# Re-cutting a routing pass into segments of 6, 5, 5, 5 and 3 blocks beside an attention kernel's half blocks

## The chip, the cores and the metric

The program runs on one core of one Trainium2 chip. The metric is the device time of one execution in microseconds, given as the median of a few executions. A core has five engines with in-order queues of their own: TensorE (PE in the profile, with its weight loads as PEld), VectorE (DVE), ScalarE (ACT), GpSimd (POOL) and SyncE (SP, which here only issues DMAs). They wait for each other through semaphores.

## The reference

The reference is a windowed attention followed by a mixture of experts. What the change touches is the routing between the two:

```python
logits = x @ w_gate
noisy_logits = logits + np.log1p(np.exp(x @ w_noise)) * noise
top2 = np.argpartition(-noisy_logits, 2, axis=1)[:, :2]      # two of 8 experts per token
for e in range(E):
    for k in range(2):
        mask = top2[:, k] == e
        h = np.maximum(x[mask] @ w1[e], 0.0)
        out[mask] += top2_w[mask, k, None] * (h @ w2[e])
```

There are 3072 tokens of 512 features (4 batches of 768, with 8 heads of 64), 8 experts and 1024 inner features.

## The kernel before

Attention goes over 24 blocks of 128 tokens. A block is done in two half blocks of four heads each, so there are 48 half blocks; half block 0 is the first. In each of them the main loop emits, in this order: `score` of the next half block (L837 on VectorE, then the exponentials L840 on ScalarE), the transposes of the attention weights (L853 on TensorE, the first TensorE work of a half block, by which the text tells them apart), `gate_t` in even half blocks (GpSimd's copies L235 of the block's finished rows, and TensorE's transposes L371), the next score products (L823), `norm` (L885, L887, L890 on VectorE), `attend` (L874 on TensorE) and `gate_l` (L393 on TensorE). A block's gate logits are ready two blocks after its attention.

Routing is a generator, `route(r)`, one for each segment of blocks in `SEG`. It is a chain of some forty short VectorE operations on tiles of at most 128x96: softplus, top two (L479, L481), one-hot marks of the chosen experts, then a running count on TensorE. The count takes, for each block of the segment, a product with a strictly upper triangular matrix (L526) and one product with ones for each earlier block (L528), and one more per block for the total (L530). From the count come each token's row and tile within its expert. `mask(i)` makes two 128x128 0/1 matrices for block i (L555), `marks(i)` makes two 128x168 tables of token number and weight (L583, one for each of the two choices), and L608 multiplies the two into PSUM; L611 adds that to the table `tab`, from which expert token lists are read.

The steps of these generators are put between the attention's instructions by `tick`, which is called seven times in a half block (four times inside `score`, three times inside `norm`) and takes one step each time, and by `finish` at the end of the half block, which takes up to five steps of the third segment (`CLOSE` = 2) and later ones, and up to three of the first two. A step that yields True, 2 or LAST keeps the generator waiting until a later place. The third segment closes expert 0's first 512 rows: as soon as it is done, four gathers (L243, GpSimd) fetch these tokens, GpSimd copies them into whole words (L235, tile `xg`), and `turn` transposes them (L338) for expert 0's first products (L1107). Segments 3 and 4 are finished among those products: the generator `late` (segment 3) and `last` (segment 4) are advanced at 32 fixed slots of expert 0's first layer, and after them `rank` sorts the experts and starts the next gathers. Masks are made by GpSimd up to the third segment and by VectorE after it.

## Time and profile before

| | us |
|---|---|
| median of 3 runs (718.05 to 721.97) | 720.09 |
| the profiled execution | 719.72 |
| its span, first to last instruction | 718.0 |

| engine | busy us | share of the span |
|---|---|---|
| PE | 692.9 | 97% |
| PEld | 618.7 | 86% |
| DVE | 456.1 | 64% |
| ACT | 439.3 | 61% |
| POOL | 320.0 | 45% |

The attention's half blocks fill the span from 7 us to about 160 us. Expert 0's first layer begins at 165 us, and the other seven experts follow from 242 us to the end. TensorE's granted clock is 1.00 of full speed all through the attention. A matmul's record lasts longer than its share of TensorE, since matmuls overlap: what a run of them costs is read from start to start.

### The profile page before, as it was taken

How to read it: one execution, taken by the hardware profiler on the slowest of the kernel's cores; microseconds unless marked ns; L12 is line 12 of the kernel's file. 1: busy time of each engine (PE TensorE's matmuls, PEld its weight loads, DVE VectorE, ACT ScalarE, POOL GpSimd, SP SyncE). 2: the span in 40 equal slices, each digit the busy share in tenths (PEclk: the TensorE clock that was granted, in tenths of full speed). 3: DMA queues.
4: the chain of work that ended last, by engine and by line, in shares of the span. 5: the costliest groups of instructions: out<-in, count | busy, mean ns of one | idle time of the engine just before them, and what ended most of it. 6: DMA issues, size and time to landing. Idle time of an engine off the chain costs nothing.

```text
span 718.0 us, 16228 instructions
## 1 busy us (share of the span) xinstructions
PE 692.9 (97%) x5769; PEld 618.7 (86%) x5769; DVE 456.1 (64%) x1473; ACT 439.3 (61%) x922; POOL 320.0 (45%) x416
## 2 busy tenths in 40 slices
PE   7999999999999799999899999999999999999995
PEld 5888888787789699999799999999899899889984
DVE  7669888967946467736563676567466756756600
ACT  6888787653328397546664586478558646845511
POOL 3363626472087371064517461644465344533222
PEclk9999999999999999999999999999999999999998
DMA  9986779684098783156915692668458646943233
GB/s 257 345 259 219 215 234 297 194 304 182 0 253 176 167 141 118 16 114 167 202 30 98 172 225 45 133 170 167 75 126 193 128 107 167 206 73 89 31 45 47
DMA packets 129913, 111.10 MB, mean 155 GB/s; under 512 B 51578, under 2 KB 96762, under 8 KB 129824
## 3 DMA queue, kind: packets, MB, share of 16 engines
q1 hardware_dynamic: 118416, 83.84, 42.3%
q0 software_dynamic: 11264, 25.89, 19.8%
q8 instruction: 47, 0.77, 0.5%
q10 hardware_dynamic: 144, 0.26, 0.2%
q14 instruction: 42, 0.34, 0.1%
HBM read 71.07 MB, written 27.59 MB: 137 GB/s over the span
## 4 chain that ended last, share of the span: by engine, by line
PE 69%; DVE 8%; issue 8%; POOL 6%; DMA 5%; ACT 3%; POOLq 0%; SPq 0%; ACTq 0%; DVEq 0%
PE bank L1397 23%; PE av L1144 20%; PE av L1167 7%; PE av L874 4%; PE sc L823 4%; PE at L853 3%; DMA xt<-xg 2%; PE at L1107 1%; POOL out_dram L1120 1%; POOL xt L235 1%; DVE wall L196 1%; DVE ns L837 1%; POOL xg L243 1%; DMA xg<-xd,ids 1%; PE sc L1107 1%
## 5 line engine op out<-in xcount | busy, mean ns | idle before, releaser
L1397 PE MATMUL bank<-xh,wall 128*128 128x384 f32 (+4 forms) x784 | 215.6, 343 | 0.2
L1397 PEld LDWEIGHTS bank<-xh,wall 128*128 128x128 f32 x784 | 143.5, 188 | 5.0 <-DVE wall L196 1.6
L1397 PE MATMUL bank<-xl,wall 128*128 128x384 f32 (+4 forms) x392 | 133.4, 340 | 0.0
L1144 PE MATMUL av<-w2h,hh 128*128 128x512 f32 x304 | 120.3, 396 | 4.8 <-ACT hh L1088 2.5
L1120 POOL DMA_INDIRECT out_dram<-y,ids x40 | 64.0, 1599 | 126.0 <-ACT y L1117 122.3
L1144 PE MATMUL av<-w2h,hl 128*128 128x512 f32 x304 | 119.4, 393 | 0.1
L1144 PE MATMUL av<-w2l,hh 128*128 128x512 f32 x304 | 119.1, 392 | 0.0
L196 DVE TENSOR_TENSOR wall<-raw,wall 128x512 fp32r<-128x512 f32 (+1 forms) x84 | 73.6, 882 | 48.4 <-ACT wall L195 48.2
L1092 DVE SCALAR_TENSOR_TENSOR hl<-bank,hh 128x384 fp32r<-128x384 f32 (+4 forms) x84 | 47.1, 561 | 64.0 <-ACT hh L1088 62.9
L195 ACT ACTIVATE wall<-raw 128x512 fp32r<-128x512 f32 (+1 forms) x84 | 58.2, 701 | 43.4 <-POOL raw L1252 43.4
L243 POOL DMA_INDIRECT xg<-xd,ids x53 | 56.6, 1067 | 52.5 <-DVE place L293 32.4
L840 ACT ACTIVATE a<-ns,mx 128x168 f32<-128x168 f32 (+1 forms) x192 | 67.9, 422 | 19.4 <-DVE mx L837 18.7
L1397 PEld LDWEIGHTS bank<-xl,wall 128*128 128x128 f32 x392 | 73.9, 188 | 2.7
L1144 PEld LDWEIGHTS av<-w2h,hh 128*128 128x128 f32 x304 | 57.1, 188 | 14.8 <-ACT hh L1088 3.0
L1144 PEld LDWEIGHTS av<-w2h,hl 128*128 128x128 f32 x304 | 57.1, 188 | 13.3 <-DVE hl L1092 0.8
L275 ACT ACTIVATE xg<-xt 128x1024 uint16<-128x1024 uint16 (+3 forms) x46 | 59.4, 1312 | 11.7 <-DMA xt<-xg 11.7
L1144 PEld LDWEIGHTS av<-w2l,hh 128*128 128x128 f32 x304 | 57.1, 188 | 9.4 <-DVE w2l L196 0.3
L837 DVE CUSTOM_DVE_ANT_0 ns<-sc,bias 128x168 f32<-128x168 f32 (+1 forms) x188 | 51.7, 318 | 18.5 <-PE sc L823 13.5
L1251 POOL TENSOR_TENSOR raw<-raw 128x256 f32<-128x256 f32 x28 | 21.8, 779 | 90.3 <-DVE wall L196 90.2
L1088 ACT ACTIVATE hh<-bank 128x384 fp32r<-128x384 f32 (+4 forms) x84 | 42.0, 500 | 31.3 <-DVE bank L1467 23.8
L235 POOL COPY xt<-y 128x256 uint16<-128x256 uint16 x96 | 35.2, 404 | 50.8 <-DVE y L890 50.8
L874 PE MATMUL av<-vs,at 128*64 128x65 f32 (+1 forms) x768 | 57.3, 224 | 0.0
(214 smaller groups left out, 1484.4 us busy)
## 6 DMA issues: line engine op xcount, KB each, us to landing
raw<-in_w SPq DMA_DIRECT2D x64, 256.0 KB
raw<-in_w SPq DMA_DIRECT2D x32, 512.0 KB
out_dram<-zero SPq DMA_DIRECT2D x14, 512.0 KB
vs<-in_v SPq DMA_DIRECT2D x24, 260.0 KB
xd<-xt SPq DMA_DIRECT2D x24, 256.0 KB
qbuf<-in_q SPq DMA_DIRECT2D x23, 256.0 KB
ks<-in_k SPq DMA_DIRECT2D x20, 272.0 KB
vp<-in_v SPq DMA_DIRECT2D x20, 195.0 KB
```

The costliest lines, as they stand in the source:

```text
L195: nc.scalar.activation(hi, src, AF.Copy)
L196: eng.tensor_sub(lo, src, hi.bitcast(F32))
L243: nc.gpsimd.indirect_dma_start(out=xg[e, t].bitcast(U16)[:m], out_offset=None, in_=xd[:n], in_offset=bass.IndirectOffsetOnAxis(ap=r, axis= ...
L275: nc.scalar.activation(words(x), xt.pop((e, t)).rearrange("p (h k) t -> p h (k t)", h=2), AF.Copy)
L837: nc.vector.tensor_tensor_reduce(out=ns[x][:, s, :w], in0=ps[:, s], in1=bias[:, u + x, s] if i else bias0[:, u + x, s], scale=-scale, scal ...
L840: nc.scalar.activation(A[n + x][:, s * w:(s + 1) * w], ns[x][:, s, :w], AF.Exp, bias=mx[x][:, s:s + 1], scale=-1.0)
L874: nc.tensor.matmul(ps[s * Q:(s + 1) * Q, h], a[r:z, part * P + q0:part * P + q0 + Q], t[r:z, c], start=k == 0 and (n == 1 or h == 0), stop ...
L1092: nc.vector.scalar_tensor_tensor(lo, src, 0.0, hi.bitcast(F32), op0=OP.max, op1=OP.subtract)
L1120: ins = nc.gpsimd.indirect_dma_start(out=out, out_offset=bass.IndirectOffsetOnAxis(ap=r, axis=0), in_=y, in_offset=None, bounds_check=N + ...
L1144: nc.tensor.matmul(ps, x[j][:, f, cols], w[:, f], start=n == 0, stop=n == 3 * FC - 1)
L1167: nc.tensor.matmul(to, w[:, f, cols], x[:, f], start=n == 0, stop=n == 3 * FC - 1)
L1397: nc.tensor.matmul(ps, wb[c % 2][u][:, 2 * a + k], x[v][:, 2 * b + k], start=start and n == 0, stop=stop and n == 5, skip_group_check=True)
```

## The change

1. The segments are 6, 5, 5, 5 and 3 blocks instead of 6, 6, 5, 4 and 3. The second and the third segment end one block (two half blocks) earlier; the fourth has one block more.
2. A cap, `PACE`, is set back at the start of each half block: at most 4 steps of segment 0, 5 of segment 1 and 8 of segment 2 are taken in it, by `tick` and `finish` together. Segments 3 and 4 have no cap.
3. The count takes one product with the triangular matrix over all blocks of the segment and then, for d = 1 to w, one product with ones whose output is shifted by d blocks: 1 + w products for a segment of w blocks, whose outputs grow to 48 columns.
4. `marks(i)` makes both tables of a block in one operation of 128x336.
5. The first three segments have one group of marks each (all masks, all marks, then all products), where the first two had two groups of three blocks. All masks come before the wait for the marking of the segment before, and the ring of masks has 12 buffers instead of 5. The third segment's masks are made by VectorE instead of GpSimd.

```diff
-    SEG = [(0, 6), (6, 12), (12, 17), (17, 21), (21, NT)]
+    SEG = [(0, 6), (6, 11), (11, 16), (16, 21), (21, NT)]
...
-        for i in range(w):
-            nc.tensor.matmul(pos[:, i], upper, ohs[:, i], start=True, stop=i == 0)
-            for j in range(i):
-                nc.tensor.matmul(pos[:, i], ones, ohs[:, j], start=False, stop=j == i - 1)
-        for j in range(w):
-            nc.tensor.matmul(tot, ones, ohs[:, j], start=j == 0, stop=j == w - 1)
+        of = ohs.rearrange("p t e -> p (t e)")
+        nc.tensor.matmul(ps[:, :w * E], upper, of, start=True, stop=False, skip_group_check=True)
+        for d in range(1, w + 1):
+            nc.tensor.matmul(ps[:, d * E:(w + 1) * E], ones, of[:, :(w + 1 - d) * E], start=False, stop=d == w,
+                             skip_group_check=True)
...
-            m = wts.tile([P, 2, P], FR, name="m", bufs=5)
+            m = wts.tile([P, 2, P], FR, name="m", bufs=12)
-                (nc.vector if r > CLOSE else nc.gpsimd).tensor_scalar(m[:, j], iota_p, row[:, i, j:j + 1], None,
+                (nc.vector if r >= CLOSE else nc.gpsimd).tensor_scalar(m[:, j], iota_p, row[:, i, j:j + 1], None,
...
-        size = w if r == CLOSE else 3
+        size = w if r <= CLOSE else 3
...
-            cs = [P, 3 * E, TT]
-            for j in range(2):
-                what = ev[:, i, j].rearrange("p x e -> p (x e)")[:, :, None]
-                nc.vector.tensor_tensor(c[:, j], what.to_broadcast(cs),
-                                        band[:, i, j][:, None, :].to_broadcast(cs), op=OP.mult)
+            cs = [P, 2, 3 * E, TT]
+            what = ev[:, i].rearrange("p j x e -> p j (x e)")[:, :, :, None]
+            nc.vector.tensor_tensor(c, what.to_broadcast(cs), band[:, i][:, :, None, :].to_broadcast(cs), op=OP.mult)
...
+        if r <= CLOSE:
+            for i in range(w):
+                mask(i)
+                yield True if r < CLOSE and i % 2 else None
+            while marking:
+                yield True
+        marking.append(r)
         for x, gr in enumerate(groups):
+            for i in gr:
+                if r <= CLOSE:
+                    marks(i)
+                    yield 2 if i == w - 1 else True if i % 2 else None
...
+        PACE = {0: 4, 1: 5, 2: 8}
+        left = {}
         def begin():
+            left.update(PACE)
...
         def go(y):
             x = y[0]
+            left[y[1]] = left.get(y[1], 99) - 1
...
-                if y[0].ready <= place:
+                if y[0].ready <= place and left.get(y[1], 1) > 0:
```

On VectorE, half block 17, in which the first segment's softplus is computed, from the last operation of `score` to the end of the half block, before (L837 is `score`; L885, L887 and L890 are `norm`; the rest is routing):

```order
L837 ISA ns,mx<-sc,bias 128x168
L837 ISA mx 128x1
L465 SCALAR_TENSOR_TENSOR aside<-aside 128x48
L885 TENSOR_SCALAR den<-av 128x4
L465 SCALAR_TENSOR_TENSOR aside<-aside 128x48
L887 RECIPROCAL den<-den 128x4
L467 SCALAR_TENSOR_TENSOR aside<-aside 128x48
L890 TENSOR_TENSOR y_98<-av,den 128x256
L469 SCALAR_TENSOR_TENSOR aside<-aside 128x48
L471 TENSOR_TENSOR aside<-aside,noise_s 128x48
L473 TENSOR_TENSOR aside<-aside 128x48
L479 MAX aside<-aside 128x8
```

The same stretch now (line numbers behind the count are lower by one to seven):

```order
L835 ISA ns,mx<-sc,bias 128x168
L835 ISA mx 128x1
L465 SCALAR_TENSOR_TENSOR aside<-aside 128x48
L883 TENSOR_SCALAR den<-av 128x4
L885 RECIPROCAL den<-den 128x4
L888 TENSOR_TENSOR y_98<-av,den 128x256
```

The steps inside `score` stay (the last of its four is the first L465 here), and the six behind it move to later half blocks.

On GpSimd, from the third segment's masks to the whole-word copies of expert 0's four gathered tiles (`xt<-y` are a block's rows, `xg<-xd` the gathers, `xg<-xg` the copies of gathered tiles), before:

```order
L555 TENSOR_SCALAR wall<-iota_p,aside 128x128 x10
L235 COPY xt<-y_98 128x2x128 x4
L243 DMA xg<-xd,ids_87 128x1024
L235 COPY xt<-y_97 128x2x128 x4
L243 DMA xg<-xd,ids_87 128x1024 x2
L235 COPY xt<-y_98 128x2x128 x4
L243 DMA xg<-xd,ids_87 128x1024
L235 COPY xg<-xg 128x2x128 x4
L235 COPY xt<-y_97 128x2x128 x4
L235 COPY xg<-xg 128x2x128 x12
```

and now:

```order
L235 COPY xt<-y_97 128x2x128 x4
L243 DMA xg<-xd,ids_87 128x1024 x2
L235 COPY xt<-y_98 128x2x128 x4
L243 DMA xg<-xd,ids_87 128x1024 x2
L235 COPY xt<-y_97 128x2x128 x4
L235 COPY xg<-xg 128x2x128 x16
```

The ten masks are gone from GpSimd. All sixteen copies of gathered tiles now stand behind the last but one block's rows, where four of them stood ahead of it.

On VectorE, the half block into which the third segment's masks now go:

```order
L554 TENSOR_SCALAR wall<-iota_p,aside 128x128 x2
L835 ISA ns,mx<-sc,bias 128x168
L835 ISA mx 128x1
L554 TENSOR_SCALAR wall<-iota_p,aside 128x128 x2
L883 TENSOR_SCALAR den<-av 128x4
L577 TENSOR_TENSOR xg<-aside 128x336
L885 RECIPROCAL den<-den 128x4
L577 TENSOR_TENSOR xg<-aside 128x336
L888 TENSOR_TENSOR y_98<-av,den 128x256
```

where the same stretch of `norm` held these rows before, with no mask on this engine:

```order
L837 ISA ns,mx<-sc,bias 128x168
L837 ISA mx 128x1
L885 TENSOR_SCALAR den<-av 128x4
L583 TENSOR_TENSOR xg<-aside 128x168 x2
L887 RECIPROCAL den<-den 128x4
L583 TENSOR_TENSOR xg<-aside 128x168 x2
L890 TENSOR_TENSOR y_97<-av,den 128x256
L583 TENSOR_TENSOR xg<-aside 128x168 x2
```

Four pairs of masks now stand inside `score`, each ahead of the next exponential's input.

## Rows read from the trace of the kernel before

**Rows 1.** Windows: start:end and length, busy us (instructions) by engine, clock, DMA; half blocks 10 to 30.

```profile
36.00:39.50 3.50, 3.50 (x78) 3.00 (x75) 2.20 (x15) 2.26 (x7) 2.44 (x5) 1.00 1.03 337
56.92:60.50 3.58, 3.15 (x59) 2.52 (x55) 3.48 (x22) 2.71 (x7) 2.02 (x6) 1.00 0.56 162
60.50:64.78 4.28, 4.12 (x78) 3.33 (x75) 4.25 (x38) 2.95 (x7) 0.75 (x2) 1.00 0.99 330
64.78:68.18 3.40, 3.40 (x89) 3.12 (x86) 3.33 (x24) 2.82 (x10) 0.75 (x2) 1.00 0.54 167
68.18:71.21 3.03, 3.03 (x64) 2.73 (x60) 1.80 (x14) 2.73 (x9) 0.75 (x2) 1.00 0.71 216
71.21:73.83 2.62, 2.62 (x58) 2.31 (x55) 2.41 (x16) 2.10 (x7) 0.77 (x2) 1.00 0.54 181
73.83:77.33 3.50, 3.50 (x79) 3.00 (x75) 3.50 (x23) 2.31 (x7) 3.11 (x5) 1.00 0.86 228
98.02:102.21 4.19, 4.11 (x78) 3.32 (x74) 4.16 (x38) 2.94 (x7) 0.75 (x2) 1.00 0.70 209
```

**Rows 2.** Windows, same columns: half blocks 35 to 44, 36 to 42, 40, 42, 44.

```profile
114.76:151.60 36.84, 35.02 (x621) 29.22 (x617) 30.00 (x193) 24.62 (x70) 22.79 (x43) 1.00 0.73 232
118.08:143.90 25.82, 24.71 (x426) 20.52 (x425) 23.61 (x151) 17.92 (x51) 12.83 (x24) 1.00 0.70 227
130.01:134.76 4.75, 4.64 (x98) 3.85 (x95) 4.42 (x37) 3.31 (x10) 0.00 (x0) 1.00 0.86 284
137.63:143.90 6.27, 5.48 (x72) 4.36 (x69) 5.59 (x32) 4.06 (x11) 6.27 (x11) 1.00 0.06 19
146.47:151.60 5.13, 4.42 (x79) 3.39 (x75) 2.27 (x14) 2.17 (x6) 4.37 (x9) 1.00 0.99 274
```

**Rows 3.** Timeline of PE: first and last of a six-block count's 27 products.

```profile
67.49 0.20 PE L526 MATMUL lg<-aside,upper 128*128 128x8 bf16 x2
...
68.03 0.29 PE L530 MATMUL lg<-aside,ones 128*128 128x8 bf16 x6
```

**Rows 4.** Source lines of masks and marks: ns min/median/max; then L303's group.

```profile
L555 POOL TENSOR_SCALAR wall<-iota_p,aside x34: 598/660/884, 74.2 to 143.1; 128x128 fp32r<-128x128 f32 x34
L555 DVE TENSOR_SCALAR wall<-iota_p,aside x14: 276/279/283, 172.2 to 189.8; 128x128 fp32r<-128x128 f32 x14
L303 DVE TENSOR_TENSOR xg<-perm,tab 128x343 f32<-128x343 f32 x2 | 1.6, 800 | 0.0
```

**Rows 5.** Timeline of PE: the third segment's marks, and half block 44's gate products.

```profile
141.53 1.37 PE L608 MATMUL lg<-xg,wall 128*128 128x168 f32 x8
143.14 0.35 PE L608 MATMUL lg<-xg,wall 128*128 128x168 f32 x1 [0.23 <-POOL wall L555]
...
150.27 0.38 PE L393 MATMUL m<-pair,wgn 128*32 128x128 f32 x3 [0.32 <-issue]
151.03 0.63 PE L393 MATMUL m<-pair,wgn 128*32 128x128 f32 x11 [0.39 <-issue]
```

**Rows 6.** Timeline of POOL: the masks, the last gather and the tile copies.

```profile
137.07 6.59 POOL L555 TENSOR_SCALAR wall<-iota_p,aside 128x128 fp32r<-128x128 f32 x10 [7.24 <-DVE aside L563]
...
154.44 1.03 POOL L243 DMA_INDIRECT xg<-xd,ids  x1
...
158.49 0.75 POOL L235 COPY xt<-y 128x256 uint16<-128x256 uint16 x2 [0.72 <-DVE y L890]
159.18 4.74 POOL L235 COPY xg<-xg 128x256 uint16<-128x256 uint16 x12
```

**Rows 7.** Timeline of PE: the hand-over to expert 0.

```profile
162.84 1.47 PE L338 MATMUL sc<-ident,xg 128*128 128x128 f32 x8 [0.49 <-POOL xg L235]
```

**Rows 8.** Timeline of DVE, then PE: the last marks of segment 4.

```profile
189.61 0.47 DVE L555 TENSOR_SCALAR wall<-iota_p,aside 128x128 fp32r<-128x128 f32 x2
190.00 0.57 DVE L583 TENSOR_TENSOR xg<-aside 128x168 fp32r<-128x168 f32 x2
190.87 0.90 PE L608 MATMUL lg<-xg,wall 128*128 128x168 f32 x6
```

More of the change, by code (lines that the diff above doesn't have):

```diff
@@ L522, in route @@
         ps = lgp
-        pos = ps[:, E:(w + 1) * E].rearrange("p (t e) -> p t e", t=w)
-        tot = ps[:, :E]
-        for i in range(w):
-            nc.tensor.matmul(pos[:, i], upper, ohs[:, i], start=True, stop=i == 0)
-            for j in range(i):
-                nc.tensor.matmul(pos[:, i], ones, ohs[:, j], start=False, stop=j == i - 1)
-        for j in range(w):
-            nc.tensor.matmul(tot, ones, ohs[:, j], start=j == 0, stop=j == w - 1)
+        pos = ps[:, :w * E].rearrange("p (t e) -> p t e", t=w)
+        tot = ps[:, w * E:(w + 1) * E]
+        of = ohs.rearrange("p t e -> p (t e)")
[3 more added lines that the diff above has]
+                             skip_group_check=True)
         if r != CLOSE:
@@ L563, in route @@
         nc.vector.tensor_copy(row, si)
-        if r == CLOSE and not marking:
-            marking.append(r)
-            for i in range(w):
-                mask(i)
         yield
@@ L579, in marks @@
             c = b[:, :6 * E * TT].bitcast(FR).rearrange("p (j x t) -> p j x t", j=2, t=TT)
-            cs = [P, 3 * E, TT]
-            for j in range(2):
-                what = ev[:, i, j].rearrange("p x e -> p (x e)")[:, :, None]
-                nc.vector.tensor_tensor(c[:, j], what.to_broadcast(cs),
-                                        band[:, i, j][:, None, :].to_broadcast(cs), op=OP.mult)
-            put_in[i] = put_in[i], c
-        while r <= CLOSE and marking and marking != [r]:
-            yield True
-        if r not in marking:
-            marking.append(r)
-        for x, gr in enumerate(groups):
-            if r <= CLOSE and not put_in:
-                for i in gr:
-                    mask(i)
-            for i in gr:
-                if r > CLOSE:
-                    mask(i)
-                marks(i)
-                if r == CLOSE:
-                    yield 2 if i == w - 1 else True if i == 1 else None
-                else:
-                    yield from (None, ) if r < CLOSE else (None, ) * 3
-            if r != CLOSE:
-                yield from (True, 2) if r < CLOSE else (None, ) * 3
+            cs = [P, 2, 3 * E, TT]
+            what = ev[:, i].rearrange("p j x e -> p j (x e)")[:, :, :, None]
+            nc.vector.tensor_tensor(c, what.to_broadcast(cs), band[:, i][:, :, None, :].to_broadcast(cs), op=OP.mult)
+            put_in[i] = put_in[i], c
+        if r <= CLOSE:
[5 more added lines that the diff above has]
+        marking.append(r)
+        for x, gr in enumerate(groups):
+            for i in gr:
+                if r <= CLOSE:
+                    marks(i)
+                    yield 2 if i == w - 1 else True if i % 2 else None
+                else:
+                    mask(i)
+                    marks(i)
+                    yield from (None, ) * 3
+            if r > CLOSE:
+                yield from (None, ) * 3
             ps = lgp[:, (SW + 1) * E:][:, :3 * E * TT]
@@ L797, in finish @@
                 n = 5 if y[1] >= CLOSE else 3
-                while n and y in active and y[0].ready <= END:
+                while n and y in active and y[0].ready <= END and left.get(y[1], 1) > 0:
                     go(y)
```

## The prediction

> **What bounds the kernel now.** I read the page first: TensorE is busy for 692.9 of 718.0 us, so what counts is what TensorE does and where it stands still. Then I cut the attention into its half blocks by the starts of L853 and read the windows of each, because only there does routing lie beside other work. A half block without routing takes one of three times by its place: 3.50 us with a gate product (half block 10), 3.03 without (20), 2.62 if odd (21, which has six routing instructions and needs no more for them) [rows 1]. Half blocks 17, 18 and 30 take 3.58, 4.28 and 4.19 us, and in them VectorE is busy for all but 0.1 us (4.25 of 4.28 in 18, with 38 instructions where half block 20 has 14) [rows 1]. So where routing comes in heaps, VectorE bounds the half block; where it comes thinly, it is free: half block 22 has 23 instructions, steps inside `score` among them, and its 3.50 us are those of half block 10 [rows 1]. Last I looked at the third segment, in the half blocks 35 to 44, 36.84 us in all, of which 40, 42 and 44 are far too long (4.75, 6.27, 5.13 us) [rows 2], and at the hand-over to expert 0.
>
> **The count.** Before, a segment of w blocks takes w(w-1)/2 + 2w products: 27, 27, 20, 14 and 9, together 97. Now it takes 1 + w: 7, 6, 6, 6, 4, together 29. From the first product at 67.49 to the start of the last, 5 x 0.025 after 68.03, 26 steps pass in 0.67 us, 25.6 ns each [rows 3]. The trace has no bf16 product of 48 columns. It costs at least these 25.6 ns; for the other end I take the marks' products, eight of 168 columns in 1.37 us, 0.17 each [rows 5], of which 48 columns are 0.05. The 29 products thus cost 0.74 to 1.45 us against 2.48, and I take the low end, as the columns are few. The 14 of the third segment lie in a stretch that VectorE bounds, so I count them as nothing; the other 54 give **-1.4 us** (-0.7 to -1.7).
>
> The floor under a small product has a rule too. The Trainium skill, page "TensorE: Matmul & The Clock Gate", section "Wait — 56ns, not 53.3ns?", says that matmuls start no closer than about 25 ns apart however few columns they have, with 32 columns at 25 ns. This trace agrees at 8 columns (25.6 ns); 48 columns would by the page's array clock fit under the same floor, and the sum would then be the -1.4 taken above.
>
> **The first two segments.** With the caps, at most 4 and 5 steps fall into a half block. The excess of the old ones goes: 3.58 - 2.62, 4.28 - 3.50 and 4.19 - 3.50 [rows 1] are 0.96, 0.78 and 0.69; half block 19 (3.40, and half block 31 like it) has 0.69 of count above its 2.62 and 0.09 of VectorE's. Together 2.6 us. What is late next: the second segment's marks, which now come two blocks' worth in each of half blocks 30 to 32 beside other steps. A pair of marks was 0.57 us, the next instruction 0.49 later [rows 8]. One operation of 336 elements isn't in the trace: from below it costs the second half of a pair again with no new start, about 0.42; from above L303's 0.80 for 343 elements [rows 4]. I take 0.45, since the pair itself, which streams the same elements, leaves VectorE after 0.49. Four of them in two half blocks, beside three or four short steps, go over VectorE's 1.2 us of free time (3.03 - 1.80 [rows 1]) by a few tenths: I add 0.3. **-2.3 us** (-2.6 to +1).
>
> **The third segment.** Half blocks 40, 42 and 44 are 1.25, 3.24 and 1.63 us above 3.50, 3.03 and 3.50 (from the change of segments on, blocks pair otherwise, which moves gate products but not their number). Of these 6.1 us, ten marks' products (1.7) stay. So 4.4 us can go. In 42 it is GpSimd's masks: ten take 6.59 us, and TensorE's marks wait for the last of them (0.23 us twice, and the products that need 1.7 us stretch from 141.53 to 143.90) [rows 5, 6]. In 44 it is two stops of 0.3 to 0.4 us that the profile gives to no engine ("issue") [rows 5]; the change aims at nothing there, but the rest of that half block is GpSimd's lateness. What comes in: five pairs of masks on VectorE, 0.39 us each from start to start [rows 8], 1.95; and the second segment's five marks, which were half over by then: 5 x 0.45 against 3 x 0.49, 0.8; less five pairs made single, 0.2. VectorE is already busy for 23.61 of the 25.82 us of half blocks 36 to 42 [rows 2], and with 8 steps in each of them it has no room, so I let all of this, 2.55, and a further 0.5 for masks that stand ahead of exponentials, be seen. **-1.3 us** (-4.4, if it finds room because the segment starts two half blocks earlier; +1, if the delay inside `score` doubles).
>
> On who makes masks the Trainium skill has a rule, and first the rows: a mask takes GpSimd 598 to 884 ns, and VectorE 276 to 283 [rows 4]. The page "SBUF — State Buffer", section "SBUF: two separate sides", says that GpSimd and VectorE share one pair of ports, which a VectorE operation with two SBUF inputs locks for its whole length; the spread of GpSimd's masks beside marks fits that, and VectorE's own durations show nothing of it. By the rule the move would cost GpSimd nothing that it isn't rid of, and the sum stays.
>
> **The hand-over.** In order, the fourth gather stays where it was, but the first tile's four copies no longer fill the time before the last but one block's rows (158.49): sixteen copies follow those rows instead of twelve. Twelve take 4.74 us from 159.18 [rows 6], four more 1.58. TensorE's last transposes already wait for these copies (0.49 us at 162.84 [rows 7]), and expert 0's first product needs all four tiles. Nothing covers it: **+1.6 us** (0, if TensorE comes later than I think; 2.1, if a gather lands late too).
>
> **Expert 0's first layer.** Segment 4's last marks end at 190.49 on VectorE and TensorE's six products follow at 190.87 [rows 8]: VectorE is the one that is late there. The fourth segment's fifth block adds a pair of masks and a mark, 0.39 + 0.45, and a pair of max operations, and six pairs of marks become single, 0.04 each or a little more. What lies ahead of the first evictions is hidden by VectorE's waiting. **+0.5 us** (0; +2.4 if a mark costs L303's 0.80). `rank` and the gathers behind it move with it and add nothing.
>
> **The sum.** -1.4 - 2.3 - 1.3 + 1.6 + 0.5 = -2.9 us. The profiled execution took 719.72 us (its span 718.0 and 1.7 around it), 0.37 under the median, so I predict 720.09 - 2.9 = **717.2 us**.
>
> **Rivals.** (A) The third segment's stall goes whole: starting at half block 35 instead of 37 and capped at 8, it fits into free time, and the -1.3 become -4.4: 714.1 us. For it: half block 22 took 23 instructions free of charge [rows 1], and VectorE idles for 2.9 of the 5.13 us of half block 44 [rows 2]. Against: VectorE's 23.61 of 25.82 us.
> (B) VectorE's gains are given back: a mark costs 0.80, which adds 0.35 for each of some sixteen that lie in stretches which VectorE bounds or ends, 5.6 at most and about half of it seen: 720.0 us. For it: L303 is the only operation of that size and kind [rows 4]. Against: the pair's 0.49.
> (C) Slower: caps spread routing over some 28 half blocks (15 to 45, less those that only wait), and in nearly all of them the steps now sit inside `score`, ahead of the inputs of the exponentials. Four short steps there are about 0.4 us (the six above half block 20's 1.80 in half block 21 are 0.6 of VectorE's time [rows 1]); if TensorE's transposes wait for that in each, it is up to 11 us. From 0.25 us a half block on it beats the gains and 0.5%; at 0.3 the time is 717.2 + 8.4 = 725.6. Against: half block 22, again.
> The change could also fail to do what it says, if the caps delay the closing so far that gathers come after attention; the order puts the fourth at the same place, so I leave that in the hand-over's bound.
>
> **How the numbers follow.** Forecast 45% (715 to 719.5), A 28%, B 15%, C 12%. About 0.5%, 3.6 us, is what a measurement of this kernel can tell from no change, so faster means under 716.5 and slower over 723.7. The forecast case lies below 716.5 in a third of its weight, A nearly always: 0.15 + 0.27 = 0.42 faster. C and a little of B: 0.12 slower. The rest, 0.46, is the same. For the range I take A's lower side, 712 (with a stop of half block 44 gone besides), and up to 722.5, into which B falls and C does not.
>
> **What would show it.** The count's runs are 7 or 6 products, 25 ns apart. Half blocks 17 to 19 and 30 fall to about 3.50, 2.62 and 3.50. The stretch of half blocks 35 to 44 is 35 to 36 us; 32.5 would mean A. The L577 rows say 0.45 or 0.80. Sixteen copies end some 6.3 us after the last but one block's rows and the first expert product waits about 1 us more for them. The forecast is wrong if half blocks with four steps inside `score` exceed 3.50, 3.03 and 2.62, or if the time after expert 0's first layer differs by more than 1 us from before.

## The result, and the profile after

The changed kernel takes 722.90 us (median of 17 runs, 720.29 to 724.08), the kernel before 717.97 on the same chip (17 runs, 714.79 to 723.87): 1.0055 times as long, 95% interval 1.0037 to 1.0074 (the ratio is taken over all the runs, so it isn't that of the two medians). Two later comparisons gave 1.0050 (1.0017 to 1.0082) and 1.0061 (1.0033 to 1.0089). So the change is slower by a little over half a per cent, about 4 us. I had forecast 717.2 us and 2.9 us faster; 722.9 lies just outside my range of 712 to 722.5.

Three profiles of the changed kernel exist (722.3, 717.7 and 720.3 us of span; "after", its second and its third) and two of the kernel before. From half block 15 to 43 the three agree to 0.02 us in each half block, and so do the two: what is read there is no chance. First the windows of the changed kernel, in the columns of [rows 1]: half blocks 17, 18, 19, 27, 30, 31, 32, 34, 38, 39, 41, and the stretch of 35 to 44.

```profile
56.78:59.66 2.88, 2.88 (x59) 2.52 (x55) 2.60 (x19) 2.88 (x9) 2.11 (x6) 1.00 0.42 115
59.66:63.29 3.63, 3.63 (x78) 3.12 (x75) 2.80 (x21) 2.35 (x6) 0.74 (x2) 1.00 1.02 322
63.29:66.00 2.71, 2.71 (x63) 2.43 (x59) 1.72 (x17) 2.58 (x9) 0.74 (x2) 1.00 0.95 323
86.09:89.53 3.44, 3.15 (x59) 2.52 (x55) 3.44 (x23) 2.82 (x8) 2.71 (x7) 1.00 0.70 171
95.86:98.92 3.06, 3.06 (x62) 2.75 (x59) 2.82 (x18) 2.92 (x10) 0.74 (x2) 1.00 0.76 218
98.92:101.54 2.62, 2.62 (x59) 2.31 (x55) 2.55 (x14) 1.69 (x5) 0.74 (x2) 1.00 0.75 214
101.54:107.19 5.65, 5.65 (x96) 4.90 (x93) 4.11 (x27) 4.27 (x12) 0.74 (x2) 1.00 0.83 267
109.88:113.62 3.74, 3.70 (x70) 2.98 (x66) 3.44 (x27) 2.46 (x6) 0.75 (x2) 1.00 0.72 208
122.17:127.28 5.11, 3.98 (x68) 2.95 (x65) 5.11 (x38) 3.36 (x9) 1.92 (x4) 1.00 0.99 312
127.28:131.53 4.25, 4.25 (x75) 3.80 (x71) 3.18 (x21) 2.22 (x6) 0.85 (x2) 1.00 0.81 282
135.46:139.46 4.00, 3.15 (x59) 2.52 (x55) 4.00 (x24) 2.50 (x6) 0.20 (x1) 1.00 0.71 238
113.62:150.54 36.92, 33.89 (x605) 28.59 (x601) 31.19 (x193) 25.30 (x70) 14.70 (x31) 1.00 0.81 261
```

Against [rows 1], half blocks 17, 18 and 19 fall from 3.58, 4.28 and 3.40 to 2.88, 3.63 and 2.71, and 30 from 4.19 to 3.06: VectorE's excess is gone from them, as forecast. But half block 32, 3.03 us before, is 5.65: twelve marks' products, a gate product and a count stand in it. Half blocks 27 and 34 are longer too, 3.44 and 3.74. These two are compared further down. In 38 and 41 VectorE works without a pause (5.11 of 5.11, 4.00 of 4.00), where half block 38 had been 2.54. The stretch of 35 to 44, [rows 2] 36.84 us, is 36.92.

Next the starts that lead from there to the experts, in us from the span's start, each read as the first instruction's row. The profiles reach half block 15, in which the first routing step stands, at times of their own, before the change can act, so two kernels are compared from there on:

| | before | its second | after | its second | its third |
|---|---|---|---|---|---|
| half block 15 | 51.10 | 51.02 | 50.97 | 50.72 | 51.04 |
| half block 31 | 102.21 | 102.16 | 98.92 | 98.68 | 99.01 |
| half block 33 | 108.65 | 108.59 | 107.19 | 106.95 | 107.28 |
| half block 36 | 118.08 | 118.02 | 116.24 | 116.00 | 116.33 |
| half block 44 | 146.47 | 146.41 | 146.98 | 146.74 | 147.08 |
| half block 47 | 156.83 | 156.80 | 157.47 | 155.32 | 157.57 |
| first product of expert 0 | 164.99 | 164.97 | 166.62 | 164.57 | 166.72 |
| its first down product | 191.61 | 191.62 | 195.42 | 191.74 | 193.87 |
| first product of expert 1 | 245.68 | 245.21 | 249.38 | 246.30 | 247.88 |
| from there to the span's end | 472.34 | 478.09 | 472.90 | 471.39 | 472.45 |

Counted from half block 15, the changed kernel is 3.15 us ahead at half block 31 and 1.70 at 36, and 0.65 behind at 44. The hand-over (from the first transpose of a gathered tile to the first product of expert 0) then adds 1.0: it takes 5.29 to 5.40 us, and 4.31 before. From that product to the first down product it is 26.62 and 26.65 us before, and 27.17 and 27.15 in the second and third profile of after: 0.5 more. Two more things come in some executions only. One is the "issue" stop of [rows 5] in half block 44 (1.5 us there): it came in both profiles of before; of after it came in the first and third, in half block 45 (3.92 us, where the second has 2.75), and not in the second. Here it is on VectorE, in the first profile:

```profile
151.84 0.16 DVE L883 TENSOR_SCALAR den<-av 128x4 f32<-128x4 f32 x1 [1.61 <-PE at L851]
```

The other is TensorE's granted clock. Windows of the hand-over and of the 5 us behind it: of after, the first profile, and then of its third.

```profile
161.32:166.62 5.30, 4.35 (x39) 2.54 (x35) 3.17 (x10) 2.67 (x5) 5.30 (x15) 1.00 0.20 75
166.62:171.62 5.00, 5.00 (x22) 3.82 (x22) 4.11 (x32) 0.80 (x2) 0.27 (x1) 0.66 0.79 292
```

```profile
161.42:166.72 5.30, 4.36 (x37) 2.54 (x34) 3.17 (x10) 2.67 (x5) 5.30 (x15) 1.00 0.20 74
166.72:171.72 5.00, 5.00 (x34) 3.65 (x35) 4.03 (x32) 1.53 (x4) 0.28 (x1) 1.00 0.78 290
```

The waits ahead are the same (4.35 and 4.36 busy of 5.30); behind them the clock is at its lower level, 1.2 GHz, for 3.41 us in one and at 2.4 GHz in the other, which passes 34 products instead of 22. The first layer's first part (its up products) takes 27.49 us in the one and 25.82 in the other (25.88 before): 1.6 us by chance. The third profile has such a stretch of 3.41 us too, and so has the second, but ahead of expert 1's first product, from 239.77 and 237.38 us.

The small steps, in timelines of after: the twelve marks' products and the count of half block 32 on PE, the tile copies on POOL, the marks' products at the first layer's end on PE (answers to [rows 3], [rows 6] and [rows 8]), and the source lines of marks and masks (to [rows 4]).

```profile
105.61 1.57 PE L601 MATMUL lg<-xg,wall 128*128 128x168 f32 x12
107.03 0.19 PE L526 MATMUL lg<-aside,upper 128*128 128x40 bf16 x1
107.07 0.27 PE L528 MATMUL lg<-aside,ones 128*128 128x40 bf16 x5
107.19 0.64 PE L851 MATMUL at<-ident,a 128*128 128x128 f32 x4
```

```profile
159.28 6.27 POOL L235 COPY xg<-xg 128x256 uint16<-128x256 uint16 x16
```

```profile
194.68 0.90 PE L601 MATMUL lg<-xg,wall 128*128 128x168 f32 x6 [0.58 <-DVE tab L604]
195.42 0.43 PE L1142 MATMUL av<-w2h,hh 128*128 128x512 f32 x1
```

```profile
L577 DVE TENSOR_TENSOR xg<-aside x24: 477/504/704, 96.5 to 193.9; 128x336 fp32r<-128x336 f32 x24
...
L554 POOL TENSOR_SCALAR wall<-iota_p,aside x22: 591/600/650, 83.7 to 119.4; 128x128 fp32r<-128x128 f32 x22
```

The six products of the count (40, 40, 32, 24, 16 and 8 columns) take 0.16 us from the first start to the next work's, 27 ns each; in the trace the second start is 38 ns behind the first, and the steps after it are 25 ns. The floor of about 25 ns that the Trainium skill, page "TensorE: Matmul & The Clock Gate", section "Wait — 56ns, not 53.3ns?", states holds for 40 columns too. A mark of 336 elements takes 0.50 us where the pair of 168 took 0.57, not 0.80. The twelve marks' products take 1.42 us from the first start to the count's, 0.12 each.

In the eighteen profiles of all the kernels here, expert 0's first product starts 1.06 to 1.21 us after GpSimd's last copy of a gathered tile (165.55 and 166.62 us above), except with the cut alone, whose copies end long before. So GpSimd's copies set the end of the hand-over.

### The profile page after: what moved, and what is told of

It is laid out like the page before. It is cut to its first block, busy times and chain, and to the rows that moved or that the text cites. A ratio compares the mean times of both kernels' runs of the same rounds, so it can differ in the third digit from the quotient of the medians.

```text
span 722.3 us, 16072 instructions
## 1 busy us (share of the span) xinstructions
PE 694.0 (96%) x5705; PEld 618.1 (86%) x5705; DVE 455.5 (63%) x1459; ACT 439.4 (61%) x923; POOL 311.0 (43%) x404
## 3 DMA queue, kind: packets, MB, share of 16 engines
q0 software_dynamic: 11264, 25.89, 19.1%
## 4 chain that ended last, share of the span: by engine, by line
PE 52%; DVE 14%; issue 13%; DMA 7%; ACT 6%; POOL 6%; POOLq 0%; SPq 0%; ACTq 0%; DVEq 0%
PE bank L1395 16%; PE av L1142 16%; PE av L872 5%; PE sc L821 4%; PE at L851 4%; DMA xt<-xg 3%; DMA xg<-xd,ids 3%; DVE wall L196 3%; PE av L1165 3%; ACT hh L1086 2%; DVE w2l L196 2%; POOL out_dram L1118 2%; ACT xh L195 1%; POOL xg L243 1%; POOL raw L1250 1%
## 5 line engine op out<-in xcount | busy, mean ns | idle before, releaser
L835 DVE CUSTOM_DVE_ANT_0 ns<-sc,bias 128x168 f32<-128x168 f32 (+1 forms) x188 | 53.8, 320 | 20.6 <-PE sc L821 11.8
```

The lines of the kernel that those rows point to most:

```text
L835: nc.vector.tensor_tensor_reduce(out=ns[x][:, s, :w], in0=ps[:, s], in1=bias[:, u + x, s] if i else bias0[:, u + x, s], scale=-scale, scal ...
```

## The experiments

My theory after the result: the loss is late (the hand-over and what follows), and in the third segment VectorE is the bound. The rivals: the cut into segments, the caps, the masks on VectorE, the grouping of marks. Times stand beside runs of the kernel before on the same chip. Starts are compared from half block 15 on, as above.

**The first tile's copies, moved ahead (kernel after).**
```
-                yield LAST
-            for t in range(TA):
+                yield LAST if t < TA - 1 else whole_words(0, 0) or LAST
+            for t in range(1, TA):
```


> The kernel after the change, with one thing moved: the first of expert 0's four tiles is copied to whole words right behind the fourth gather, so twelve copies instead of sixteen follow the rows of the last but one block, as before the change. Everything else, on every engine, stands as in the kernel after. Theory 1 (the late hand-over costs twice, once as a wait for the copies and once because the wait is followed by a stretch at half of TensorE's clock): the first product of expert 0 starts about 1.0 us earlier than in the kernel after (164.6 against 166.6 less what attention itself is later, 0.65), the granted clock stays at 1.00 behind it, and the first layer's first part ends 2.0 to 2.7 us earlier (191.5 to 192 instead of 194.1); time 720.2 to 721. Theory 2 (VectorE with the fourth segment's routing sets the end of the first layer): the start moves by 1.0 and the end by less than 0.6; time as the kernel after, 722.5 to 722.9.

Measured: 719.93 us, before 717.39, 1.0041 (1.0012 to 1.0070); the time doesn't tell it from the kernel after. The hand-over takes 4.89 us instead of 5.30 (before: 4.31); the clock stayed at 1.00 behind it and the first part took 25.89. So the late copies cost 0.4 us of the 1.0. The rest goes with later gathers: the last one starts 0.98 us ahead of half block 47 (2.39 before), and from it to the last copy GpSimd now works without a pause. The 1.6 us I put down to this edit were the clock's chance, as the next profiles of after show.

**The new count alone (part 3 of the change, its diff as above), and the new cut alone (kernel before).**
```
-    SEG = [(0, 6), (6, 12), (12, 17), (17, 21), (21, NT)]
+    SEG = [(0, 6), (6, 11), (11, 16), (16, 21), (21, NT)]
```


> The kernel before the change with the count by shifted products alone (97 products become 29). My prediction's term: the 54 products fewer of the four segments that VectorE doesn't bound save 1.4 us (0.7 to 1.7), all by the end of the first layer, of which 1.0 by the end of half block 35 (segments 0 and 1): half blocks 19 and 31 fall from 3.40 to about 2.85, and the time to 716.5. Rival: the count lies beside VectorE's work or shifts the waits only, and attention ends within 0.3 us of before; time 718.

> The kernel before the change with the new cut into segments alone (6, 5, 5, 5, 3 blocks instead of 6, 6, 5, 4, 3). Theory A (the fifth block of the fourth segment makes VectorE late in expert 0's first layer, and sixteen copies after the last but one block's rows make the hand-over late): half blocks 35 to 44 are not slower than before, the first product of expert 0 starts 0.5 to 1.5 us later, the first layer ends 2 to 3 us later than before, and the time is 720 to 721. Theory B (the new cut is harmless and the caps or VectorE's masks do the harm): the first layer ends within 0.8 us of before, and the time is 717.5 to 718.5.

Measured: the count 716.09, before 717.39, 0.9980 (0.9955 to 1.0006). Half blocks 19 and 31 are 2.90; half block 36 starts 1.00 earlier, 44 1.35 earlier: in the trace the term of 1.4 us was right, and the time can't show it. The cut 718.19, 1.0006 (0.9977 to 1.0034). Its half block 44 starts as before. Its gathers start 6.5 to 8.8 us sooner (138.82 to 145.63 us; before 145.35 to 154.44) and its copies are done at 155.26, and the hand-over still takes 4.25 us, about what it takes before. In its first layer TensorE waits for VectorE twice, 0.75 us for the last segment's count and 0.84 for its last marks' products, and the layer takes 28.09 us to the first down product (26.62 before). The cut by itself does no harm that the time can show: theory B.

**The closing segment without its cap, its masks on GpSimd, two groups of marks, no cap at all (kernel after).**
```
-        PACE = {0: 4, 1: 5, 2: 8}
+        PACE = {0: 4, 1: 5}                      (first; {} in the last)
-                (nc.vector if r >= CLOSE else nc.gpsimd)...
+                (nc.vector if r > CLOSE else nc.gpsimd)...   (second)
-        size = w if r <= CLOSE else 3
+        size = w if r == CLOSE else 3                        (third)
```


> The kernel after the change without the cap of 8 steps a half block on the closing segment (the third); the caps of 4 and 5 on the first two stay. Theory A (what half blocks 37 to 41 lose comes from the second segment's marks and VectorE's masks meeting there, not from the cap): half blocks 35 to 44 stay within 0.7 us of the kernel after (36.9 us in all), the order of GpSimd and of the queues doesn't change, so the hand-over stays; time 722.5 to 723.5. Theory B (the cap stretches the closing over too many half blocks, each of which pays): the stretch falls by 1.5 us or more and attention ends as much earlier; time 720.5 to 721.4.

> The kernel after the change with the closing segment's ten masks back on GpSimd (VectorE makes those of the last two segments only, as before). Theory 1 (VectorE is the bound in half blocks 37 to 41, so 2.8 us of masks off it shorten them): the stretch of half blocks 35 to 44 falls from 36.9 us to 35.5 or less; GpSimd's ten masks, 6 us, now stand half blocks ahead of the marks' products and stall nobody; the hand-over and the half clock behind it stay; time about 1.5 us under the kernel after, 720.5 to 721.5. Theory 2 (GpSimd's masks stall TensorE as they did before the change, in a half block of 6.27 us): the stretch stays at 36.9 or grows; time 722.9 to 725.

> The kernel after the change with the marks of the first two segments in two groups of three and two or three blocks again, as before. Theory 1 (one group of twelve products with six marks on VectorE ahead of them makes one half block of 5.65 us, which eats what the caps had gained, 4.1 us at half block 32): half block 32 falls to about 3.5 to 4 us, and half block 36 starts 1.0 to 2.0 us earlier than in the kernel after (116.24); of this at most half is left at the end of attention, since the order of the closing segment's marks moves too, and since the gathers stand half a block later or earlier by it; time 721 to 722. Theory 2 (the products and marks cost the same in two halves, only spread): half block 36 starts within 0.4 us of 116.24.

> The kernel after the change without any cap (the steps of a segment go as fast as the places in a half block let them, as before the change). In this order GpSimd copies four tiles' parts ahead of the last but one block's rows and twelve behind, as before. Theory 1 (the caps earn 1 us or more in the first two segments, by half block 28, and cost the late hand-over): half block 28 starts 0.7 to 2.0 us later than in the kernel after (89.53), the first product of expert 0 comes 0.5 us or more earlier after the last attention than the 5.3 us of the kernel after, the clock stays at 1.00 behind it, and the time is 718.5 to 720.5. Theory 2 (the caps' gain is all real and the rest of the change does the harm): time 723.5 to 725.

Measured, with the length of half blocks 36 to 43 (30.74 us in after, 28.39 before):

- Without the closing cap 720.39, before 717.39, 1.0030 (1.0008 to 1.0053), length 30.59. The cap isn't it. The stretch of 35 to 44 is theory A's; the time, under theory A's, isn't clear of after's.
- Masks on GpSimd 719.14, before 716.45, 1.0038 (1.0009 to 1.0066), length 29.35: theory 1 in the trace; the time doesn't tell it from after's (1.0050 on the same chip). This is half block 41 in it, where after has 4.00 us:

```profile
135.65:138.26 2.61, 2.61 (x57) 2.31 (x54) 2.61 (x16) 2.34 (x8) 2.61 (x6) 1.00 0.58 163
```

TensorE waits for nothing, and GpSimd's ten masks stall nobody: in the new order they start at 134.08 and their products stand in half block 43, which begins at 141.89. VectorE's masks alone cost 1.39 us of these half blocks.

- Two groups: 726.72, before 716.45, 1.0120 (1.0077 to 1.0164). Half block 32 is shorter, 3.79, but 31 is 3.60, and half block 36 starts 0.29 later than in after: theory 2, the grouping gains nothing. Its gathers start some 5 us later (154.23 to 161.08 us; after 148.87 to 155.89); the hand-over takes 6.92 us, the clock stands at the lower level for 10.24 us from 163.77 on, and expert 0's first product comes at 169.56.
- No cap: 724.67, before 716.45, 1.0102 (1.0068 to 1.0136), theory 2's time. Half block 28 starts 3.08 us later than in after, but 36 only 0.71 and 44 only 0.59 later: what the caps gain early is nearly all given back. My 718.5 to 720.5 missed in part because the hand-over didn't shorten (5.75 us), and in part with the clock: its mean is 0.991 in the timed runs (after: 0.994; two groups: 0.989).

**The same kernels again (nothing edited).**

> The kernel after the change once more, with nothing changed, for a second profile. What is to be told apart: the stretch at half of TensorE's clock behind the hand-over (from 167.2 us, 3.41 us long) and the stop of 1.2 us in half block 45 stand in one profile only so far. Theory: the stretch at half clock comes back at the same place, because the wait for the tile copies ahead of it does; the stop in half block 45 does not come back (three kernels with the same instructions up to there, or nearly the same, show 2.75 us for it instead of 3.92). Rival: both are chance, and the first layer's first part then takes 25.9 us here as in the kernel before. Time 721 to 723.

> The kernel before the change once more, with nothing changed, for a second profile. Theory: the two stops in half block 44 (5.13 us in the profile that I predicted from) are chance, as the same half block took 3.63 us in the kernel before with the new count; it takes 3.6 us here, and attention ends 1.5 us earlier (half block 47 at 155.3 instead of 156.83). So does the half clock at 358.1 us with TensorE's stop of 2.5 us ahead of it not come back there. Rival: the stops belong to the kernel before, and half block 44 takes 5 us again. Time 716.5 to 718.

> The kernel after the change once more, for a third profile. Theory: half blocks 12 to 43 are those of the other two profiles to 0.02 us each, the hand-over takes 5.3 to 5.4 us, and whether the half clock follows it is chance: if it does, the first layer's first part takes 27.5 us, if not 25.9. Time 1.004 to 1.006 of the kernel before.

Measured: after 720.53 (before 716.45) and 722.47 (before 717.52), with the ratios above; before again 719.29 (the kernel before's other runs there 718.62), 0.9984 (0.9950 to 1.0018). Where my theories spoke of chance, some fell. The half clock isn't behind the hand-over in the second and third profile of after, so its place isn't set by the kernel; 3.41 us of it stand ahead of expert 1 there. In the kernel before it stands at 358.11 us in one profile, and at 425.16 and 561.70 in the other. The stop of half block 44 came back in the kernel before, 5.15 us, to my surprise. The half blocks agree from 15 on, not from 12.

**Other sets of parts (kernel before).** With the count: new cut and caps 4 and 5 ("first"); old cut and caps 5 and 6 ("second"); marks of a block in one operation ("third", and once more). The rest of the cap, the cut and the count are as in the diffs above.
```
+        PACE = {0: 4, 1: 5}                      (first; {0: 5, 1: 6} in the second)
...
-            cs = [P, 3 * E, TT]
+            cs = [P, 2, 3 * E, TT]               (third: one tensor_tensor for both j)
```


> The kernel before the change with three of the change's parts: the new cut into segments, the count by shifted products, and caps of 4 and 5 on the first two segments. Masks, marks and their groups stand as before the change. Theory 1 (the harm in the third segment is in the marks and masks, one group a segment and VectorE's masks): half blocks 36 to 44 take 32.3 us or less (34.1 in the kernel after), half block 45 starts at 148 to 149, the hand-over takes 4.3 to 4.6 us, and the time is 715.5 to 717. Theory 2 (caps push the second segment's work into the closing segment's half blocks, whoever makes masks): half blocks 36 to 44 take 33 us or more, and the time is 718 to 720.

> A version that may beat both: the kernel before the change with the count by shifted products and with caps of 5 and 6 steps on the first two segments (of 6 blocks each, the old cut). GpSimd keeps the order 4 copies, rows, 12 copies. Theory 1 (a cap only takes VectorE's excess out of half blocks 17, 18 and 30): 0.5 to 1.5 us less than the kernel before with the count alone (716.1 on another chip's run, 1.3 under before), attention ends about as much earlier. Theory 2 (what the caps take out comes back when the marks of the second segment meet the closing one): attention ends at or after that of the count alone (half block 45 at 148.96), and the time is that of the count alone or up to 1 us more.

> The kernel before the change with the count by shifted products and with the marks of one block in one operation of 336 elements instead of two of 168; masks, groups, caps and cut as before the change. Theory 1 (the longer operation is cheaper, 0.41 us from start to start against 0.49 to 0.57 for the pair): with the count alone as the measure, half blocks with marks are 0 to 0.2 us shorter each, attention ends 0 to 0.5 us earlier, the first layer is shorter by 0.2 to 0.4; time 0.3 to 0.8 under the count alone. Theory 2 (a long operation ahead of the exponentials' inputs delays them): attention ends 0.3 us or more later.

> The kernel before the change with the count by shifted products alone, once more: attention up to half block 44 as in its first profile, 1.14 us under the kernel before; half block 44 either 3.6 us or, with the stops, 5.1. Time 0.998 of the kernel before (717 where that takes 718.5); rival: 1.000.

> The kernel before the change with the count by shifted products and the marks of a block in one operation, once more: attention 1.48 us under the kernel before at half block 44, the first layer shorter by 0.3 to 0.6. Time 0.9975 of the kernel before; rival (the marks' 0.5 us is not to be seen in the time): 0.999 or as the count alone.

Measured: first 723.16, before 718.62, 1.0054 (1.0019 to 1.0090); second 723.69, 1.0083 (1.0052 to 1.0114). The first fits neither theory: its half blocks 36 to 44 take 32.63 us, between the two, and its time is above both. Its loss comes earlier, in half block 27:

```profile
86.25:92.22 5.97, 4.27 (x58) 3.49 (x54) 5.87 (x36) 3.71 (x10) 5.52 (x13) 0.79 0.31 84
```

The first segment's marks meet the second's softplus there, VectorE is busy for 5.87 of 5.97 us (the half block takes 2.76 with the count alone), TensorE waits for 1.7 us, and from 89.69 on its clock is at the lower level for 3.41 us. So a part of this loss is the clock's. The second is theory 2 in kind and beyond it in size (half block 45 at 156.11, where the theory had 148.96 or a little later), with the clock at 1.00 all through the attention. Windows of the second: half blocks 18, 28, 29, 42; then half blocks 28, 29 and 42 of the count alone, without caps.

```profile
60.36:63.99 3.63, 3.63 (x79) 3.12 (x75) 2.89 (x24) 2.35 (x6) 0.74 (x2) 1.00 1.00 307
...
92.50:96.69 4.19, 3.58 (x62) 2.95 (x59) 4.05 (x24) 2.89 (x8) 0.74 (x2) 1.00 0.64 196
96.69:100.82 4.13, 3.85 (x64) 3.26 (x61) 4.04 (x31) 3.45 (x10) 0.81 (x2) 1.00 0.41 117
...
140.89:148.42 7.53, 5.49 (x73) 4.37 (x69) 6.63 (x36) 4.06 (x11) 6.83 (x11) 1.00 0.09 34
```

```profile
92.05:95.11 3.06, 3.06 (x63) 2.76 (x59) 2.96 (x18) 2.81 (x9) 0.74 (x2) 1.00 0.45 125
95.11:97.73 2.62, 2.62 (x59) 2.32 (x55) 2.52 (x16) 1.89 (x5) 0.74 (x2) 1.00 0.99 278
...
136.49:142.76 6.27, 5.48 (x73) 4.37 (x69) 5.60 (x32) 4.06 (x11) 6.27 (x11) 1.00 0.23 85
```

Half block 18 has its 0.65 us less; 28 and 29 then hold the first segment's late marks beside the second segment's steps and are 1.13 and 1.51 longer, and 42 is 1.26 longer. It is 1.7 us behind the count alone at half block 36 and 5.7 at 44.

The third: 716.85, before 718.62, 0.9976 (0.9948 to 1.0003); again 716.22, before 717.52, 1.0000 (0.9974 to 1.0027). The count alone again: 718.03, 1.0003 (0.9980 to 1.0026). In the traces the count and joint marks together are 1.7 us ahead of before at half block 44 in both profiles, and 2.3 and 2.7 at the first down product; the time doesn't show it beyond doubt. It is the best version found; that it beats the kernel before is not shown.

**Both places undone (kernel after: masks on GpSimd and the first tile's copies ahead).**

> The kernel after the change with both places undone that were found to lose: the closing segment's masks are made by GpSimd again, and the first tile's four copies stand ahead of the last but one block's rows. Theory 1 (the two are additive): attention ends as in the kernel after with GpSimd's masks alone (half block 45 at 149.2), half block 41 takes 2.62 us, the first product of expert 0 starts at about 163.2 (163.62 with GpSimd's masks alone), the first layer's first part takes 25.9 us, and the time is within 0.3% of the kernel before, 1.0 to 1.0035 times it. Theory 2 (most of the loss is elsewhere, in the experts behind): the trace moves so, and the time stays 0.4% or more above the kernel before.

Measured: 725.60 of 6 runs, before 717.52, 1.0102 (1.0074 to 1.0130). Theory 1's time is missed, and theory 2's (0.4% or more above) holds. The profiled run, 720.38, is as theory 1 says up to the last half blocks (half block 41 2.62, 45 starts at 149.56, the first part 25.86), but the stop came in half block 45 (3.90), so the first product comes at 165.12. With the stop on both sides, that is 0.2 us ahead of before, and the first down product is 0.3 to 0.4 behind: up to there, undoing the two places takes nearly all of the loss out of the trace. The time it doesn't give back. The other five runs take 723.29 to 726.67 at mean clocks of 0.988 to 0.992, and the one with a profile 0.997: by (1 - clock) x 2 x the time these five spend some 11 to 17 us at half clock (the profiled one 4.6, at its end), and where cannot be seen without a profile.

## Why the prediction was wrong

**The count (-1.4): right,** in the trace. Alone it gives 1.00 us by half block 36, 1.35 by 44 and 1.6 by the first down product (in its second profile, which has the stop as the kernel before).

**The first two segments (-2.3): the first step that failed.** They gave nothing. At half block 36 the lead is 1.70 us; the count is 1.00 of it, and six marks' products fewer made by then, at 0.12 each, are 0.74. The excess of half blocks 17, 18 and 30 did go, about 2.0 us. I then asked what is late next and added 0.3. But the caps take no work away: they put it off, and it came back as 2.1:

- Half block 32 holds the first segment's twelve products, done in 23 and 25 before. Of its 5.65 us, 3.50 are a half block with a gate product, 1.42 the products and 0.16 the count; 0.57 is loss.
- In half block 27 the second segment's softplus now stands, and VectorE is busy throughout: 3.44 us, and 2.77 before. In 34 it is 3.74 against 3.23 with the cut alone. These are the other kernels' windows, before and then the cut alone:

```profile
89.58:92.35 2.77, 2.77 (x61) 2.59 (x57) 1.93 (x14) 2.63 (x9) 0.75 (x2) 1.00 0.95 296
```

```profile
111.89:115.12 3.23, 3.23 (x68) 2.73 (x67) 2.83 (x15) 1.68 (x4) 2.53 (x5) 1.00 0.62 187
```

- Half blocks 20, 21, 28, 29 and 33 add 0.03 to 0.13 each, 0.4 together.

I priced the marks that arrive, not the half blocks in which everything arrives, and I took the wrong ones: the marks in half blocks 30 to 32 are the first segment's; the second's come in 37 to 39, beside the closing segment. Against the run without caps, the caps are worth 0.71 us at half block 36; what takes that away again beside the count's 1.00 no run separates. In the kernel before with the new count, caps lose 1.7 us by half block 36 and 5.7 by 44.

**The third segment (-1.3): the step that failed by most; the sign was wrong.** Half blocks 36 to 43 take 2.35 us more. 1.39 of that is VectorE's masks (the run with them on GpSimd); the other 1.0 I put down to what stands there more of the second segment, ten marks' products instead of six (0.5 at 0.12 each) and their marks on VectorE, four of which take 0.69 to 0.70 us beside GpSimd's copies; no run separates that. I let 2.55 us of new work be seen, against a stall of 4.4 that was to go. GpSimd's stall did go, but masks that start early enough do that on GpSimd too; and the 1.63 of half block 44 is a stop of several engines that the change only moves: after has it in half block 45, or not at all. I had called the rest of that half block GpSimd's lateness without a row that said so.

Two readings of mine were wrong as well. I took 0.17 us for a marks' product from the length of eight overlapping records; from start to start it is 0.12, so ten are 1.2 us and not 1.7. And VectorE's durations do show GpSimd beside it: in the kernel before, seven of the 34 marks of 168 beside GpSimd's masks take 410 to 501 ns, and all 14 without a mask beside them 321 to 330.

**The hand-over (+1.6): right in kind, 1.0 measured.** The sixteen copies take 6.27 us, as forecast. But moving four of them back gave 0.4 us only; the rest goes with gathers that start later. What I didn't see is that half of TensorE's clock can follow such a wait.

**Expert 0's first layer (+0.5): right** in size, 0.5 measured. It shows as two waits of TensorE for VectorE, 0.57 us for the last segment's count (185.65) and 0.58 for its last marks' products (194.68); before it waited 0.23 us, and its count took longer. The cut alone has both waits.

**The rivals.** A fell with the third segment, B with the mark's 0.50 us. C was right in its sign: half blocks 28, 29, 31 and 35 take 3.63, 2.71, 2.62 and 2.62, where 3.50 and 2.62 are those without routing, so steps inside `score` cost 0.13 us at most in these, but 0.7 and 0.5 in 27 and 34; what costs is a few half blocks, those and the ones where segments meet. No rival of mine was "work put off comes back in one place", though the order of the instructions showed the marks' new place.

**What stays open.** The traces put 2.3 us of the loss in places (attention 0.8 and the hand-over 1.0 with the stop on both sides, the first layer 0.5). The times say 3.6 to 4.4. The rest is behind expert 0 or in executions that no profile shows. Behind expert 0, single executions of one kernel differ by 6 us (472.34 and 478.09; the longer one has two stretches of half clock there, the shorter has one), and the two profiled executions of before are themselves 1.8 and 6.4 us above the medians of the runs on their chips, so two or three profiles cannot find it. Nor does undoing both places bring the time back. The mean half clock is not it: in the two comparisons that have both, the mean granted clock of the timed runs is 0.9946 and 0.9952 for after and 0.9949 and 0.9948 for before.

## What to carry to other kernels

A cap on steps moves work and removes none: before counting the gain of the stretch that it empties, find the stretch where the work lands, and count there everything that meets. Masks should be made by an engine with time to spare as long as they are early enough; in the traces the stall was their late start, not their engine. A stop to which a profile gives no cause, or a lead read at one point where less work has been done, is no term of a sum. Compare two profiles from a common start, the last one ahead of the change: here that moved a lead by up to 0.5 us.

## What the runs showed that was not expected

Behind the same wait at the hand-over (5.30 us, TensorE busy for 4.35) the granted clock fell to 0.50 for 3.41 us in one profile of a kernel and not in another. Behind hand-overs of 5.29 to 5.40 us it fell in two of five profiles, each time for 3.41 us; without caps (5.75 us) it fell for 3.41, with two groups (6.92 us) for 10.24, and behind the other eleven, of 4.11 to 4.91 us, in none. Seventeen of the eighteen profiles have at least one such stretch of 3.41 or 10.24 us before the end, fourteen of them with a start between 235 and 247 us, where expert 1 begins. What one costs depends on its place: 1.6 us behind the hand-over, and little where expert 1 begins (first down product to expert 1: 53.96 us without one in the first profile of after, 54.56 and 54.01 with one in the other two).

In timed runs the mean clock is 0.989 with two groups, 0.991 without caps and with both places undone, 0.992 to 0.995 in all others. At the 1.6 us for 3.41 that after shows, my estimate for the lower clock is 3.8, 2.7 and 2.4 us in those three, a part of their loss of 7 to 10 us.

VectorE, ScalarE and TensorE stop at 148 to 156 us, beside a gather's issue on GpSimd, in nine of eighteen profiles: all three stand for 0.2 to 0.4 us at a time, and the half block takes 1.2 to 1.6 us more; no wait of an instruction names a cause. The other nine issue the same gathers without it.

GpSimd's masks, 598 to 884 ns before, take 591 to 650 in after and 590 to 733 with the closing ones among them. The long ones stand beside VectorE's marks. But a mask with marks over all of its 842 ns (at 82.20 us, before) takes only 0.24 us longer than the shortest, and one with marks of 336 over 608 of its 617 ns (at 136.39, with the closing masks on GpSimd) 0.03 longer. The Trainium skill, page "SBUF — State Buffer", section "SBUF: two separate sides", says that on the shared ports one engine holds the pair for its whole instruction and the other is blocked; by these records the two engines do hinder each other, but by less than that. It decided nothing here.
